# Expert tiles of a routed layer moved from a stage of their own into the chunks of a gated recurrence

## The chip, the cores and the metric

The kernel runs on one core of one Trainium2 chip. The metric is the device time of one execution in microseconds, lower is better. Five engines work beside each other, each through its own instructions in a fixed order: TensorE (PE in the profile, with its weight loads shown as PEld), VectorE (DVE), ScalarE (ACT), GpSimd (POOL) and SyncE (SP). SP and ACT start plain transfers, POOL starts those whose rows are picked by a list of indices; 16 DMA engines carry them all.

## The reference

A gated linear recurrence feeds a routed two-expert layer. For each of 4 batches and 8 heads, over 768 steps with head size 48:

```python
state = alpha[:, :, t, :, None] * state + einsum('bhd,bhe->bhde', k[:, :, t], v[:, :, t])
y[:, :, t] = einsum('bhd,bhde->bhe', q[:, :, t], state)
```

The result is laid out as x with 3072 rows (tokens) of 384. Then, with 8 experts of hidden size 1024:

```python
noisy = x @ w_gate + log1p(exp(x @ w_noise)) * noise      # 3072 x 8
top2, weights = two largest per row, softmax over the two
out[row] = sum over its two experts e: weight * (relu(x[row] @ w1[e]) @ w2[e])
```

All in float32.

## The kernel before

**Recurrence.** The 3072 rows are 24 chunks of 128 steps, six to a batch. For a chunk, `prepare` turns alpha, k and q so that steps lie along the free axis (12 transposes, line 197), takes the running product of alpha with a scan (line 211), and scales q by it and k by its reciprocal (lines 214 to 218). `scores` multiplies k and q within the chunk (line 230), keeps the lower triangle (line 232) and turns k back (line 236). `finish` carries the state from chunk to chunk (lines 247 to 257), forms y (lines 260 and 265), stores its 128 rows to `x_rows` in DRAM and turns y for the router (`put_x`). The loop runs ahead of itself: in round n stand `load(n+3)`, `prepare(n+2)`, `scores(n+1)` and `finish(n)`.

**Router.** After every third chunk, which closes a unit of 384 rows (8 units), `router` works out the two experts of each row, their weights, and the place of each row in its expert's list: `rank` (lines 515 and 516) counts how many earlier rows chose the same expert. It writes six groups of 128 entries of 16 bytes (row number, weight, two further row numbers) into `table` in DRAM with transfers from POOL (line 527). Each expert owns 3072 rows of the table. A row number of 6144 means "none", and the whole table is filled with it at the start (`clear_table`, one transfer on ACT's queue). `half_rows` in DRAM holds the first of a row's two results until the second arrives, and is filled with zeros at the start (`clear_half`, eight transfers on SP's queue).

**Plan.** After the last chunk, `plan_tiles` turns the eight counts into a list of 55 tiles of up to 128 rows: for each its expert and its first place in the table.

**Experts.** Then 55 tiles run one after the other. For a tile, SP reads the expert's number and the place from the plan and loads 128 table entries (`tab`) and the expert's w1 (1.5 MB, three buffers); POOL gathers the rows of x (`gather_x`, line 596, four buffers); PE turns them (`turn_x`, line 603), forms the hidden layer in two halves (line 616: 24 products, each shown as two records), and the output (line 623: 8 products); ACT scales it by the row's weight. In `combine` POOL fetches the stored halves (line 635), stores first halves (line 641) and writes finished rows (line 649). All of w2 (12 MB) stays on chip, loaded in eight transfers from round n = 2 on.

A tile framework builds the program. Its list scheduler sets the order of each engine's instructions from the order in the source and from when operands should be ready, and it places all waits; no order is written by hand. Stages that are opened one after the other with their own buffer pools share memory, and here the experts' pools open after the recurrence's have closed. At the end a branch, not taken with this data, redoes everything with a general form of the recurrence.

Of the kernel before, what the change touches and what calls it, by code (L numbers as in the profile page):

```python
# [18 lines left out]
def kernel(  # L19
# [23 lines left out]

    nc = tc.nc
# [3 lines left out]
    C = 128  # L48
# [13 lines left out]
    RMAX = N  # L62
    NTILE = (2 * N) // C + E - 1
    TROWS = E * RMAX + (E + 0) * C
    NONE = 2 * N
    RANGE = 1e-18

# [22 lines left out]
    expert_ids = const.tile([C, E], F32, name="expert_ids")  # L90
    region = const.tile([C, E], F32, name="region")
    for e in range(E):
        nc.gpsimd.memset(expert_ids[:, e:e + 1], float(e))
        nc.gpsimd.memset(region[:, e:e + 1], float(e * RMAX))
# [7 lines left out]
    tile_no = const.tile([1, NTILE], F32, name="tile_no")  # L102
    nc.gpsimd.iota(tile_no, pattern=[[1, NTILE]], base=0, channel_multiplier=0, allow_small_or_imprecise_dtypes=True)
    step_no = const.tile([1, RMAX // C], F32, name="step_no")
    nc.gpsimd.iota(step_no, pattern=[[C, RMAX // C]], base=0, channel_multiplier=0,
# [6 lines left out]
    nothing = const.tile([C, TROWS // C * 4], U32, name="nothing")  # L112
    nc.gpsimd.memset(nothing, NONE)
    zeros = const.tile([C, NT // 8, DM], F32, name="zeros")
    nc.gpsimd.memset(zeros, 0.0)

    def clear_table():
        nc.scalar.dma_start(out=table.rearrange("(p r) w -> p (r w)", p=C), in_=nothing)

    def clear_half():  # L120
        for i in range(8):
            nc.sync.dma_start(out=half_rows.rearrange("(i n p) d -> i p n d", i=8, p=C)[i], in_=zeros)

    NIN = 3
# [28 lines left out]
    def put_x(n, y, on, ps_tp, xT, at):  # L153
        y_sb = on.tile([C, DM], F32, name="y_sb")
        nc.scalar.copy(y_sb, y.rearrange("p h d -> p (h d)"))
        tp = ps_tp.tile([C, NP, C], F32, tag="tp", name="tp")
        for a in range(KO):
            nc.tensor.transpose(tp[:, a, :], y_sb[:, ds(a * C, C)], ident)  # L158
        nc.scalar.copy(xT[:, :, ds(at * C, C)], tp[:, 0:KO, :])
        nc.sync.dma_start(out=x_rows[ds(n * C, C), :], in_=y_sb)  # L160


    def fast_gla(es, after):
        gc = pool("gc", 1, es)
        vp = pool("vp", 4, es)
        kp = pool("kp", 2, es)
        sp = pool("sp", 2, es)
        xtp = pool("xtp", 2, es)
        rp = pool("rp", 2, es)
        ps_sc = pool("ps_sc", 1, es, space=PS)  # L170
        ps_tp = pool("ps_tp", 3, es, space=PS)
        ps_y = pool("ps_y", 3, es, space=PS)
        ins = {x: [gc.tile([C, H, DP], F32, name=f"{x}_in{i}") for i in range(NIN)] for x in "akq"}
# [4 lines left out]
        a_s = [gc.tile([C, NP, C + 1], F32, name=f"a_s{i}") for i in range(2)]  # L178
        P_s = [gc.tile([C, NP, C + 1], F32, name=f"P_s{i}") for i in range(3)]
        for t in a_s:  # L180
            nc.vector.memset(t[:, :, 0:1], 0.0)
        least = gc.tile([C, NP, C + 1], F32, name="least")
        nc.vector.memset(least, RANGE)
        nc.vector.memset(least[:, :, 0:1], 1.0)
        P_end = gc.tile([C, NT, NP], F32, name="P_end")
        above = gc.tile([C, NT], F32, name="above")
        less_1 = gc.tile([C, 1], F32, name="less_1")
        nc.vector.memset(less_1, -1.0)
        MTs = [gc.tile([C, 2, NP, C], F32, name=f"MT{i}") for i in range(2)]
# [3 lines left out]

        def transposed(src):
            tp = ps_tp.tile([C, NP, C], F32, tag="tp", name="tp")
            for j in range(NP):
                nc.tensor.transpose(tp[:, j, :], src[:, 2 * j:2 * j + 2, :], ident)  # L197
            return tp

        def prepare(n):  # L200
            c = chunks[n]
            a_t = transposed(ins["a"][n % NIN])
            nc.scalar.copy(a_s[n % 2][:, :, 1:C + 1], a_t)  # L203
            over_1 = kp.tile([C, NP, C], F32, name="over_1")
            nc.scalar.activation(over_1, a_t, AF.Relu, bias=less_1, accum_out=above[:, n:n + 1])
            k_t = transposed(ins["k"][n % NIN])
            k_raw = kp.tile([C, NP, C], F32, name="k_raw")
            nc.scalar.copy(k_raw, k_t)
            q_t = transposed(ins["q"][n % NIN])
            P = P_s[n % 3]  # L210
            nc.vector.tensor_tensor_scan(P.rearrange("p j t -> p (j t)"), a_s[n % 2].rearrange("p j t -> p (j t)"),  # L211
                                         least.rearrange("p j t -> p (j t)"), 0.0, op0=ALU.mult, op1=ALU.max)
            c["q"] = kp.tile([C, NP, C], F32, name="q_P")
            nc.vector.tensor_mul(c["q"], q_t, P[:, :, 1:C + 1])
            over = kp.tile([C, NP, C], F32, name="over")
            nc.vector.reciprocal(out=over, in_=P[:, :, 1:C + 1])  # L216
            c["k"] = kp.tile([C, NP, C], F32, name="k_P")
            nc.gpsimd.tensor_tensor(c["k"], k_raw, over, op=ALU.mult)  # L218
            nc.gpsimd.tensor_copy(out=P_end[:, n, :, None], in_=P[:, :, C:C + 1])
            c["end"] = kp.tile([C, NP, 2], F32, name="end")  # L220
# [3 lines left out]
        def scores(n):  # L224
            c = chunks[n]
            sc = [ps_sc.tile([C, NP, C], F32, tag=f"sc{i}", name=f"sc{i}") for i in range(2)]
# [6 lines left out]
            if n % NCH != NCH - 1:  # L233
                tp = ps_tp.tile([C, NP, C], F32, tag="tp", name="tp")
                for j in range(NP):
                    nc.tensor.transpose(tp[:, j, :], c["k"][:, j, :], ident)  # L236
                c["k_end"] = kp.tile([C, NP, C], F32, name="k_end")
                nc.scalar.copy(c["k_end"], tp)

        def finish(n, xT, at):  # L240
            c = chunks.pop(n)
            first, last = n % NCH == 0, n % NCH == NCH - 1
            y = ps_y.tile([C, H, D], F32, tag="y", name="y")
            if not last:
                s1 = ps_y.tile([C, NP, 2, D], F32, tag="y", name="s1")
                for j in range(NP):
                    nc.tensor.matmul(s1[:, j], c["k_end"][:, j, :], c["v"][:, 2 * j:2 * j + 2, :], start=True,  # L247
                                     stop=True)
                S_new = kp.tile([C, NP * 2, D], F32, name="S_new")
                end = c["end"].rearrange("p j i -> p (j i)")[:, :, None].to_broadcast([C, NP * 2, D])  # L250
                s1 = s1.rearrange("p j i d -> p (j i) d")
                if first:
                    nc.vector.tensor_mul(S_new, s1, end)
                else:
                    S_sum = kp.tile([C, NP * 2, D], F32, name="S_sum")
                    nc.vector.tensor_add(S_sum, chunks["S"], s1)
                    nc.gpsimd.tensor_tensor(S_new, S_sum, end, op=ALU.mult)
            if not first:
                for j in range(NP):
                    nc.tensor.matmul(y[:, 2 * j:2 * j + 2, :], c["q"][:, j, :], chunks["S"][:, 2 * j:2 * j + 2, :],  # L260
                                     start=j == 0, stop=False, skip_group_check=True)
# [5 lines left out]
            if not last:  # L267
                chunks["S"] = S_new
            put_x(n, y, sp, ps_tp, xT, at)

        def load(n):
            chunks[n] = {"v": load_chunk(n, ins, vp)}

        load(0)
        load(1)
        prepare(0)
        load(2)
        prepare(1)
        scores(0)
        for n in range(NT):  # L280
            if n + 3 < NT:
                load(n + 3)
            after(n)
            if n + 2 < NT:
                prepare(n + 2)
            if n + 1 < NT:
                scores(n + 1)
            if n % UC == 0:
                xT = xtp.tile([C, KO, UT], F32, name="xT")
            finish(n, xT, n % UC)  # L290
            if n % UC == UC - 1:
                router(n // UC, xT, rp, ps_y)


        out_of = rp.tile([C, 4], F32, name="out_of")
        nc.vector.tensor_reduce(out=out_of[:, 0:1], in_=P_end.rearrange("p n j -> p (n j)"), axis=mybir.AxisListType.X,
                                op=ALU.min)
        nc.vector.tensor_reduce(out=out_of[:, 1:2], in_=above, axis=mybir.AxisListType.X, op=ALU.max)
        nc.vector.tensor_scalar(out=out_of[:, 2:3], in0=out_of[:, 0:1], scalar1=2 * RANGE, scalar2=None, op0=ALU.is_lt)
        nc.vector.tensor_scalar(out=out_of[:, 3:4], in0=out_of[:, 1:2], scalar1=0.0, scalar2=None, op0=ALU.is_gt)  # L300
        count = ps_y.tile([C, 2], F32, tag="y", name="count")
        nc.tensor.matmul(count, ones, out_of[:, 2:4], start=True, stop=True)
        again = rp.tile([1, 1], F32, name="again")
        nc.vector.tensor_reduce(out=again, in_=count[0:1, :], axis=mybir.AxisListType.X, op=ALU.add)
        nc.vector.tensor_copy(out=again_i, in_=again)
        plan_tiles(rp, ps_y)


    def general_gla(es):
# [4 lines left out]
        sp = pool("g_sp", 2, es)  # L314
# [407 lines left out]
```

## Time and profile before

| | |
|---|---|
| time, median of 3 runs | 980.18 us (979.2 to 986.29) |
| the profiled execution | 982.83 us, of which its span is 981.1 us |
| TensorE busy | 879.0 us, 90% of the span |
| VectorE, ScalarE, GpSimd busy | 268.1, 200.4, 347.9 us |
| mean granted TensorE clock | 0.866 |
| recurrence, router and plan | from 0 to about 370 us |
| 55 expert tiles | from about 370 to 971 us |

The profile cuts the span into 40 slices of 24.5 us and gives the busy share of each engine in tenths, and likewise the TensorE clock that was granted. Groups of instructions are named by line, engine and operation, output tile, input tiles. A table by windows gives, for each stretch, the busy time of each engine with the number of its instructions in brackets, the granted clock, the share of the DMA engines' time and the GB/s.

### The profile page before, as it was taken

Reading aid. Unit: us, or ns where it says so; the run is one execution under the profiler, and the core shown is the slowest. Engines: PE = TensorE matmul, PEld = TensorE weight load, DVE = VectorE, ACT = ScalarE, POOL = GpSimd, SP = SyncE. Lnnn points to the kernel's source line nnn. Section 1 sums busy time; section 2 is a strip of 40 time slices with the busy share of each in tenths; the row PEclk is TensorE's granted clock in tenths of the full one; section 3 lists DMA queues with packets and bytes.
Section 4 is the critical chain, followed back from the end, with each engine's and each line's share of the span. In section 5 each row is a group of like instructions: output and inputs, shape, how many; then the busy total and the mean of one; then the engine's idle time right before and its main releaser. Section 6 shows DMA issues by size and latency. Waiting matters only on the chain.

```text
span 981.1 us, 14593 instructions
## 1 busy us (share of the span) xinstructions
PE 879.0 (90%) x5393; PEld 738.9 (75%) x5393; DVE 268.1 (27%) x544; ACT 200.4 (20%) x370; POOL 347.9 (35%) x412
## 2 busy tenths in 40 slices
PE   5987879898797609999999999999999999999995
PEld 4876778797697607788788878887887788778873
DVE  7844584755855200011010101010101010101010
ACT  2412241333332201111111111111111111111110
POOL 3213143242342223344334433443444343434322
PEclk9955595676875558999999999999999999999998
DMA  9999162343410027544554555556555655665420
GB/s 236 292 371 211 32 128 56 66 97 63 84 41 9 17 74 264 210 169 157 195 203 156 172 203 192 176 176 217 193 179 185 216 196 180 198 218 168 160 66 3
DMA packets 164463, 152.85 MB, mean 156 GB/s; under 512 B 121704, under 2 KB 137755, under 8 KB 164384
## 3 DMA queue, kind: packets, MB, share of 16 engines
q1 hardware_dynamic: 144736, 127.53, 42.0%
q0 software_dynamic: 15616, 23.76, 7.2%
q10 hardware_dynamic: 4032, 0.53, 0.3%
q8 instruction: 46, 0.75, 0.3%
q14 instruction: 33, 0.27, 0.1%
HBM read 139.83 MB, written 31.57 MB: 175 GB/s over the span
## 4 chain that ended last, share of the span: by engine, by line
issue 44%; PE 22%; POOL 18%; DMA 7%; DVE 4%; ACT 2%; POOLq 1%; ACTq 0%; DVEq 0%; SPq 0%
POOL prev L635 6%; DMA half_rows<-o,tab 5%; POOL x_in L596 5%; PE y L265 5%; PE sc L230 4%; POOL out_dram L649 3%; PE tp L197 3%; PE s L247 3%; PE y L260 2%; PE lg L464 2%; POOL half_rows L641 2%; DVE over L216 1%; PE tp L158 1%; POOL table L527 1%; PE tp L236 1%
## 5 line engine op out<-in xcount | busy, mean ns | idle before, releaser
L616 PEld LDWEIGHTS h_ps<-xt,w 128*128 128x128 f32 x2640 | 304.8, 193 | 15.4 <-DVE xt L605 1.1
L616 PE MATMUL h_ps<-xt,w 128*128 128x128 f32 x2640 | 305.2, 276 | 0.7 <-DVE xt L605 0.7
L623 PE MATMUL o_ps<-w,h 128*128 x880 | 292.9, 486 | 0.0
L623 PEld LDWEIGHTS o_ps<-w,h 128*128 128x128 f32 x880 | 162.9, 190 | 102.0
L641 POOL DMA_INDIRECT half_rows<-o,tab x55 | 66.5, 1210 | 269.6 <-ACT o L634 263.4
L618 ACT ACTIVATE h<-h_ps 128x512 f32<-128x512 f32 x110 | 65.7, 597 | 265.6 <-PE h_ps L616 265.6
L648 DVE TENSOR_TENSOR both<-o,prev 128x384 f32<-128x384 f32 x55 | 30.8, 559 | 294.1 <-ACT o L634 281.3
L605 DVE COPY xt<-x_ps 128x384 f32<-128x384 f32 x55 | 30.7, 559 | 268.9 <-PE x_ps L603 268.9
L634 ACT ACTIVATE o<-o_ps,tab 128x384 f32<-128x384 f32 x55 | 32.0, 581 | 268.8 <-PE o_ps L623 268.8
L527 POOL DMA_INDIRECT table<-entry,place_u x48 | 48.7, 1015 | 104.7 <-DMA table<-entry,place_u 61.8
L216 DVE RECIPROCAL over<-P_s 128x512 f32<-128x512 f32 x24 | 80.4, 3348 | 0.6
L596 POOL DMA_INDIRECT x_in<-x_rows,tab x55 | 56.0, 1018 | 50.9 <-PE x_ps L603 38.3
L230 PE MATMUL sc<-q_P,k_P 48*128 48x128 f32 x384 | 50.7, 379 | 23.7 <-DVE den L486 10.2
L635 POOL DMA_INDIRECT prev<-half_rows,tab x55 | 58.3, 1059 | 38.4 <-DMA half_rows<-o,tab 28.4
L230 PEld LDWEIGHTS sc<-q_P,k_P 48*128 48x128 f32 x384 | 40.6, 260 | 33.3 <-issue 11.5
L265 PE MATMUL y<-vt,MT 128*128 128x48 f32 x384 | 65.5, 340 | 0.0
L265 PEld LDWEIGHTS y<-vt,MT 128*128 128x128 f32 x384 | 64.9, 262 | 0.1
L649 POOL DMA_INDIRECT out_dram<-both,tab x55 | 55.5, 1010 | 18.1 <-issue 16.5
L218 POOL TENSOR_TENSOR k_P<-k_raw,over 128x512 f32<-128x512 f32 x24 | 31.2, 1302 | 61.6 <-DVE over L216 23.5
L603 PE MATMUL x_ps<-ident,x_in 128*128 128x128 f32 x165 | 27.4, 276 | 28.5 <-DMA x_in<-x_rows,tab 28.5
L211 DVE TENSOR_TENSOR_SCAN P_s<-a_s,least 128x516 f32<-128x516 f32 x24 | 32.0, 1334 | 52.8 <-ACT a_s L203 52.7
L603 PEld LDWEIGHTS x_ps<-ident,x_in 128*128 128x128 f32 x165 | 20.1, 143 | 28.6 <-DMA x_in<-x_rows,tab 28.6
(119 smaller groups left out, 627.6 us busy)
## 6 DMA issues: line engine op xcount, KB each, us to landing
w<-in_moe_w_dram SPq DMA_DIRECT2D x63, 1536.0 KB
a_in<-in_alpha_dram SPq DMA_DIRECT2D x24, 192.0 KB
k_in<-in_k_dram SPq DMA_DIRECT2D x24, 192.0 KB
q_in<-in_q_dram SPq DMA_DIRECT2D x24, 192.0 KB
vt<-in_v_dram SPq DMA_DIRECT2D x24, 192.0 KB
half_rows<-zeros SPq DMA_DIRECT2D x8, 576.0 KB
x_rows<-y_sb SPq DMA_DIRECT2D x24, 192.0 KB
tab<-table SPq DMA_DIRECT2D x55, 2.0 KB
```

Of the source, the lines that this page charges most:

```text
L216: nc.vector.reciprocal(out=over, in_=P[:, :, 1:C + 1])
L230: nc.tensor.matmul(sc[i][:, j, :], c["k"][r, j, :], c["q"][r, j, :], start=True, stop=True)
L265: nc.tensor.matmul(y[:, h, :], MTs[n % 2][:, i, j, :], c["v"][:, h, :], start=first and h == 0, stop=h == H - 1, skip_group_check=True)
L527: nc.gpsimd.indirect_dma_start(out=table, out_offset=bass.IndirectOffsetOnAxis(ap=place_u[:, i:i + 1], axis=0), in_=entry.bitcast(U32)[:, ...
L596: nc.gpsimd.indirect_dma_start(out=x_in[i % NB], out_offset=None, in_=x_rows, in_offset=bass.IndirectOffsetOnAxis(ap=tabs[i][:, 0:1], axis=0),
L603: nc.tensor.transpose(x_ps[:, a, :], x_in[i % NB][:, ds(a * C, C)], ident)
L616: nc.tensor.matmul(h_ps[:, fo, :], w1[:, a, ds((half * FO // 2 + fo) * C, C)], xt[:, a, :], start=a == 0, stop=a == KO - 1)
L618: nc.scalar.activation(h[:, ds(half * FO // 2, FO // 2), :], h_ps, AF.Relu)
L623: nc.tensor.matmul(o_ps, h[:, fo, :], w2[:, ds(e, 1), fo, :].rearrange("p o d -> p (o d)"), start=fo == 0, stop=fo == FO - 1)
L635: get = nc.gpsimd.indirect_dma_start(out=prev[i % 2], out_offset=None, in_=half_rows, in_offset=bass.IndirectOffsetOnAxis(ap=tab[:, 3:4], ...
L641: put = nc.gpsimd.indirect_dma_start(out=half_rows, out_offset=bass.IndirectOffsetOnAxis(ap=tab[:, 2:3], axis=0), in_=o, in_offset=None, b ...
L649: put = nc.gpsimd.indirect_dma_start(out=out, out_offset=bass.IndirectOffsetOnAxis(ap=tab[:, 3:4], axis=0), in_=both, in_offset=None, boun ...
```

## The change

The expert tiles no longer wait for all counts. After each unit, `plan_tiles(u)`, some 25 small VectorE instructions, hands out a fixed number of tiles from the counts so far, always such tiles as are already full; the number (`GIVEN`) is what 8 experts must have full whatever the counts are: 0, 5, 11, 17, 23, 29, 35 after units 0 to 6, and all 55 after the last. `given` notes for each tile how many rows of each expert earlier tiles hold, so that a row's entry, which now has the other expert and the place there, tells whether the other result came first: five small VectorE instructions per tile (`gather_x`). One round of the chunk loop from n = 7 on holds two tiles, their four steps (`tile_steps`) laid between the seven steps of the chunk; 33 tiles stand in the loop, 22 after it. Recurrence and experts now live at the same time, so buffers go down: `NIN` 3 to 2, w1 3 to 2, x_in 4 to 3, transposes in PSUM 3 to 2, y in PSUM 3 to 1. `x_rows` is stored from ACT's queue. Both clears are one transfer each on ACT's queue with a source that repeats 16 and 512 bytes, 25600 and 9216 pieces. w2 is loaded from round 1 on. Entry transfers no longer wait for each other. `get_half` stands ahead of the second layer. The router's logits are formed per chunk and kept in `lgs`.

The core of the diff (new code in the order of the file):

```diff
+    EV = E + 1
+    GIVEN = [max(0, (2 * UT * (u + 1) - E * (C - 1) + C - 1) // C) for u in range(NU - 1)] + [NTILE]
...
-    nothing = const.tile([C, TROWS // C * 4], U32, name="nothing")
-    zeros = const.tile([C, NT // 8, DM], F32, name="zeros")
+    nothing = const.tile([C, 4], F32, name="nothing")
+    zeros = const.tile([C, C], F32, name="zeros")
     def clear_table():
-        nc.scalar.dma_start(out=table.rearrange("(p r) w -> p (r w)", p=C), in_=nothing)
+        cleared = nc.scalar.dma_start(out=table.bitcast(F32).rearrange("(p r) w -> p r w", p=C),
+                                      in_=nothing[:, None, :].to_broadcast([C, TROWS // C, 4]))
...
+    def put_entries(place, entry):
+        put = nc.gpsimd.indirect_dma_start(
+            out=table, out_offset=bass.IndirectOffsetOnAxis(ap=place, axis=0), in_=entry, in_offset=None,
+            bounds_check=TROWS - 1, oob_is_err=False)
+        for earlier in entries[1:] + taken:
+            tc.declare_no_dep(put.ins, earlier, reason="different rows of the table")
+        tc.add_manual_dep(put.ins, entries[0].name, AFTER, reason="the table is cleared first")
...
     def clear_half():
-        for i in range(8):
-            nc.sync.dma_start(out=half_rows.rearrange("(i n p) d -> i p n d", i=8, p=C)[i], in_=zeros)
+        nc.scalar.dma_start(out=half_rows.rearrange("(p n) (a d) -> p (n a) d", p=C, d=C),
+                            in_=zeros[:, None, :].to_broadcast([C, NT * KO, C]))
-    NIN = 3
+    NIN = 2
...
-        nc.sync.dma_start(out=x_rows[ds(n * C, C), :], in_=y_sb)
+        nc.scalar.dma_start(out=x_rows[ds(n * C, C), :], in_=y_sb)
...
+    def plan_tiles(u, on):
...
+        lo, hi, last, now = GIVEN[u - 1] if u else 0, GIVEN[u], u == NU - 1, u + 1
...
         def gather_x(i, units):
+            tab = tabs[i]
...
+            nc.vector.scalar_tensor_tensor(other, expert_ids, tab[:, 2:3], given[:, i, 0:E], op0=ALU.is_equal,
+                                           op1=ALU.mult, accum_out=before_it)
...
+            nc.vector.memset(skip[:, 0:1], 0.0)
+            nc.vector.tensor_tensor(skip[:, 1:2], tab[:, 3:4], before_it, op=ALU.is_lt)
+            nc.vector.tensor_tensor(skip[:, 2:3], tab[:, 3:4], before_it, op=ALU.is_ge)
...
+            nc.vector.scalar_tensor_tensor(wheres[i], skip, float(NONE), tab[:, 0:1].to_broadcast([C, 3]),
+                                           op0=ALU.mult, op1=ALU.add)
+            nc.gpsimd.indirect_dma_start(out=x_in[i % NB], out_offset=None, in_=x_rows[0:units * UT, :],
+                                         in_offset=bass.IndirectOffsetOnAxis(ap=wheres[i][:, 0:1], axis=0),
...
+    def tile_steps(i, do, units):
+        def first():
+            load_w1(i + 1)
+            if i + 2 < units[1]:
+                gather_x(i + 2, units[0])
+            layer1(i, 0)
+        def second():
+            layer1(i, 1)
+        def third():
+            if i + 1 < units[1]:
+                turn_x(i + 1)
+            get_half(i)
+            layer2(i, 0)
+        def fourth():
+            layer2(i, 1)
+            combine(i)
...
-        fast_gla(es, after)
-        experts(es)
+        def start_batch(u):
+            lo = GIVEN[u - 1] if u else 0
+            for i in range(lo, min(lo + 4, GIVEN[u])):
+                load_tab(i)
+            load_w1(lo)
+            for i in range(lo, min(lo + 2, GIVEN[u])):
+                gather_x(i, u + 1)
+            turn_x(lo)
...
+        for n in range(NT):
+            u = (n - 4) // UC
+            chunk = [lambda: prepare(n + 2), lambda: load(n + 3), lambda: scores(n + 1), lambda: state(n),
+                     lambda: output(n), lambda: turn_y(n), lambda: route(n)]
+            if n == 0:
+                load_router()
+                clear_table()
+                clear_half()
+            if n == 1:
+                load_w2()
+            work = []
+            if n >= 4 and GIVEN[u] > (GIVEN[u - 1] if u else 0):
+                lo = GIVEN[u - 1] if u else 0
+                if (n - 4) % UC == 0:
+                    start_batch(u)
+                part = (n - 4) % UC
+                for i in range(lo + 2 * part, min(lo + 2 * part + 2, GIVEN[u])):
+                    work += steps_of(i)
...
+            for j in range(max(len(work), len(chunk))):
+                if j < len(work):
+                    work[j]()
+                if j < len(chunk):
+                    chunk[j]()
+        for i in range(tiles, NTILE):
+            ...
```

## The prediction, made before the changed kernel was run

> **What bounds the kernel now.** I read the slices first, then windows of 5 us, then the timeline around the joint of the two stages.
>
> ```profile
> span 981.1 us, 14593 instructions
> ...
> PE   5987879898797609999999999999999999999995
> ...
> PEclk9955595676875558999999999999999999999998
> ```
>
> Slices 1 to 15 are the recurrence: TensorE is never idle long, yet at about half clock. Slices 16 to 40 (24.5 us each) are the tiles: TensorE full, at full clock. The windows show what the clock means for the recurrence; in them the columns are the stretch, its length, then busy us and count of PE, PEld, DVE, ACT, POOL, and last clock, DMA share, GB/s.
>
> ```profile
> 35.00:40.00 5.00, 5.00 (x49) 4.68 (x48) 2.73 (x5) 0.80 (x2) 2.07 (x2) 1.00 1.04 221
> ...
> 60.00:65.00 5.00, 5.00 (x26) 5.00 (x25) 1.25 (x2) 0.00 (x0) 2.16 (x3) 0.50 1.07 372
> ...
> 225.00:230.00 5.00, 0.25 (x2) 0.25 (x2) 4.93 (x29) 1.96 (x3) 1.40 (x2) 0.75 0.00 1
> 230.00:235.00 5.00, 5.00 (x25) 5.00 (x25) 2.39 (x9) 0.00 (x0) 2.06 (x3) 0.50 0.01 0
> ```
>
> Both 35 to 40 and 60 to 65 count as fully busy, but with 49 records against 26: full clock is 0.102 us a record, half clock 0.192. At 225 TensorE stands while VectorE does the router's 29 small instructions; after that wait the clock is 0.50. So the recurrence pays twice, in waits and in clock.
>
> ```profile
> 39.10 26.52 SPq L150 DMA_DIRECT2D w<-in_moe_w_dram  x8
> ...
> 338.76 0.59 PE L515 MATMUL rank<-chosen,before 128*128 128x24 f32 x2 [4.66 <-DVE entry L489]
> ...
> 369.58 0.90 PE L603 MATMUL x_ps<-ident,x_in 128*128 128x128 f32 x3 [28.50 <-DMA x_in<-x_rows,tab]
> ...
> 947.67 5.52 PE L616 MATMUL h_ps<-xt,w 128*128 128x128 f32 x48
> ...
> 958.52 5.52 PE L616 MATMUL h_ps<-xt,w 128*128 128x128 f32 x48
> ```
>
> A tile takes 958.52 - 947.67 = 10.85 us of TensorE, 55 take 597. Between the last `rank` and the first turned tile lie 30.8 us, 28.5 of them idle. And SP was held 26.5 us by eight w2 loads (12.6 MB; 33.8 us at the 372 GB/s of the window at 60): whoever issues a long transfer stands until most of it has gone.
>
> **The work itself.** All tiles are 597 us. The recurrence has about 1673 records (288 + 80 + 72 transposes, 384 + 384 + 160 + 160 + 144 products from the groups' counts), 69.7 a chunk: 7.1 us at 0.102. Were TensorE never to wait, 24 x 7.1 + 597 = 767 us. The change removes the joint and lets tile products fill the recurrence's waits; the built order of TensorE's instructions does show them alternating from round 7 on, so that it does what it says is not in doubt. The question is what new waits it brings. I go along TensorE's path.
>
> **A. Until `rank` of unit 1 (113.7 us in the trace of before): 129 us.** New here is that both clears stand in ACT's queue, ahead of the recurrence's first copies, in small pieces.
>
> ```profile
> q1 hardware_dynamic: 144736, 127.53, 42.0%
> ...
> q10 hardware_dynamic: 4032, 0.53, 0.3%
> ```
>
> The table's clear is 25600 pieces, 1600 on each of 16 engines. Queue q10 (noise and router weights, 32 bytes a piece) gives 0.25 to 0.35% of 16 x 981 us over 4032 packets, 10 to 14 ns each: 16 to 22 us. Queue q1's mean (42% over 144736) is 46 ns, as its packets are larger: 73 us as the upper end. I take 19, since size is what q10 shares with it. As SP was held by w2, ACT is held: its copies, which begin at 9.5 us in before, begin at about 30 (7.8 where the clear is issued now, 19, and some 3 for loads beside it). Three copies later the half-row clear holds it again: 4.7 MB at 372 GB/s are 13 us, and 10 us of SP's loads share the way, less what stays queued: free at 48. On SP's queue the third q load waits for these copies, and five w2 pieces (4.2 us each) stand behind it and ahead of chunk 4's alpha, which is copied by ACT at 78 instead of 40.0. From there to `rank` of unit 1 before took 113.7 - 40.0 = 74, of which the copies of chunks 5 and 6 (47.2 and 83.2) lay 36 apart, not the usual 13 (40 a unit): w2 again, 23 us that are now paid already. So 78 + 51 = 129.
>
> By the Trainium skill ("DMA: Bandwidth & Descriptors", Specifications), writes under 512 bytes are done as read and modify, which speaks against clearing in 16-byte pieces; the rows show only small reads, and the page has no price for it. If it doubled the 19 us, the sum would grow by about as much.
>
> **B. From there to the first turned tile: 150.** The chain that took 30.8 us before holds six entry transfers, each waiting for the last.
>
> ```profile
> POOL table L527 <- DMA table<-entry,place_u: 61.8, 29, 5.8
> ...
> x_in<-x_rows,tab POOLq DMA_INDIRECT x55, 6.4
> ...
> table<-entry,place_u POOLq DMA_INDIRECT x48, 3.4
> ```
>
> Issued from 342.4 to 359.2, they took 16.8; now 6 x 1.0 us. Five small VectorE steps come in (0.16 each, 0.8). 30.8 - 10.8 + 0.8 = 20.8 us, beside which TensorE has two chunks' remainders.
>
> **C and D. 16 chunks x 7.1 = 114 and 55 tiles x 10.85 = 597.** In a round stand two tiles and a chunk, 28.8 us. Hidden beside it, from the groups: VectorE 7.2 for the chunk, 2 x 1.9 for tiles with the new steps, some 3 for router and plan; POOL 2 x 4.3 transfers, 2.3 for the chunk, 2 for entries; DMA 0.53 (its share between 500 and 600) x 21.7, and 5.8 for a chunk's loads (0.56 and 0.31 of 25 us from 200 to 250, 3.75 chunks), 17 us. The `x_rows` stores leave SP, where one stood 4.2 us behind w2 at 65.7, for ACT, where an issue takes under 1 us. Each has room, so w1 in two buffers (freed after a first layer, due two half layers and a chunk later, 16 us at least, for 1.5 MB, 4.2 us) and gathers (6.4 us, issued more than a tile ahead) should arrive. The recurrence runs a round ahead of need, so its scan and reciprocal have 28 us. If that cover goes, each late gather costs its remainder to everything behind it, since one queue serves both.
>
> **E. New waits: 49.** (1) `rank`: from where ACT takes the logits, 334.14, to `rank` took 4.6 us, and now with one more copy 4.9; ahead of it stand four second-layer products (2.7). 2.2 us in each of 6 units, and 1.6 for the clock after it (the first 48 records of a tile at 371 took 7.09 us instead of 5.52): 23. (2) The last batch starts after two tiles, 21.7 us, against a chain of 20.8 behind other work of POOL: 2. (3) Small waits in a round, from fewer buffers (one y, two for transposes) and mixed queues, that no row shows: 0 to 5 us, from nothing (all operands a round early) to one `rank`-like wait; nearest are the 0 to 1 us idle entries of most groups: 1.5 x 16 = 24.
>
> **F. Tail: 12,** as before (969.2 to 981.1: last output, two transfers, the branch).
>
> Sum: 150 + 114 + 597 + 49 + 12 = 922 us of span, 924 as a profiled execution (982.8 against 981.1). The median was 2.7 below that execution, so **921 us**, 6% faster.
>
> **Rivals.**
>
> *Clock, slower than before.* If TensorE's short waits in each round keep the clock low, the shared stretch (33 tiles and 16 chunks, 472 us at full clock) grows. Against it speaks that the first tile lost only those 1.6 us; for it that 60 to 65 is fully busy and yet at 0.50. It decides once an eighth of the stretch is at half rate, 59 us. At a quarter: 921 + 118 = 1040. The skill ("TensorE: Matmul & The Clock Gate", Part 1) says that some 3.4 us of sustained work restore full clock; by that the sum loses nothing here, while the stretch from 60 to 80 us, busy at 0.50, does not follow it.
>
> *The clears hold ACT longer, or the waits move.* At 46 ns a piece the table takes 73 instead of 19 us: 975. Or every round waits 5 us, by POOL's queue, where a fetch of halves waits for the last store to land (2.6 us) ahead of gathers: 921 + 56 = 977. Either is no measurable gain.
>
> *Better.* w2 arrives while ACT is held, so A could be 15 us shorter, and E could be 15: 870.
>
> **Numbers.** Forecast (895 to 955) 0.43; better 0.17; the second rival (955 to 1000) 0.18; the clock 0.22. Within 1% is about what a measurement here can tell from no change, 970 to 990. Faster by more: 0.43 + 0.17 + 0.07 = 0.67; same 0.07; slower 0.04 + 0.22 = 0.26. Range 868 to 1025: below it lies little, above it half of the clock's rival.
>
> **What would show it.** ACT's first copy near 30 us and chunk 4's near 78; the first turned tile near 150; rounds of 29 to 31 us at a granted clock over 0.95; `rank` waits of 2 us; no idle before the last batch over 3 us; a tile at 10.85 in the last 22. Wrong if rounds take over 33 us, if the clock in them is below 0.9, or if the first copy comes after 60.

## The result, and the profile after

The changed kernel takes **1052.63 us** (1041.2 to 1056.08) against 979.69 us (976.91 to 986.29) for the kernel before on the same chip: ratio 1.0714, 95% interval 1.0616 to 1.0812. It is 7% slower, where 921 us was forecast and the range ended at 1025. The profiled execution took 1056.08 us, its span 1054.2.

First the page of the changed kernel: the span, two rows of the slices (now 26.4 us each) and the queue that carries the clears (packets, MB, share of 16 engines' span).

```profile
span 1054.2 us, 15008 instructions
...
PE   1100487988997999899799999998998799999995
...
PEclk9999755555997899899989989997999899999998
...
q10 hardware_dynamic: 42192, 9.97, 12.4%
```

In the first four slices TensorE does next to nothing. The stretch of low clock, slices 3 to 15 in the kernel before, is now slices 5 to 10, and tiles follow, so the change does what it says; but the tiles start 100 us later than forecast. Queue q10 took 0.3% of the engines' time before, and now 12.4%.

The same stretch by windows (stretch, length, then busy us and count of PE, PEld, DVE, ACT, POOL; clock, DMA share, GB/s):

```profile
25.00:50.00 25.00, 3.09 (x20) 2.50 (x20) 1.33 (x2) 0.00 (x0) 0.00 (x0) 1.00 1.81 29
50.00:75.00 25.00, 0.00 (x0) 0.00 (x0) 0.00 (x0) 0.00 (x0) 0.00 (x0) 1.00 1.33 66
75.00:100.00 25.00, 0.00 (x0) 0.00 (x0) 0.00 (x0) 0.00 (x0) 0.00 (x0) 1.00 1.56 20
```

From 50 to 100 all five engines stand. Only the DMA engines work, at a share of 1.3 to 1.8 (above 1, since the recorded times of single transfers overlap), and they move 20 to 66 GB/s; in the kernel before it was 276 GB/s over the first 100 us. What ACT and SP do meanwhile stands in their timelines (start, us, queue, line, operation; the length of an issue is how long it held its engine):

```profile
27.66 74.32 ACTq L153 DMA_DIRECT2D half_rows<-zeros  x1
102.08 0.58 ACT L242 COPY a_s<-tp 128x512 f32<-128x512 f32 x1 [93.26 <-issue]
```

```profile
29.68 10.73 SPq L167 DMA_DIRECT2D vt<-in_v_dram  x1
...
47.07 9.85 SPq L165 DMA_DIRECT2D q_in<-in_q_dram  x1
108.77 0.37 SPq L165 DMA_DIRECT2D a_in<-in_alpha_dram  x1
```

ACT's issue of the half rows' clear lasts 74.32 us, behind the table's pieces (the same 9216 pieces took 0.59 us to issue in wide_table below, where they went first). SP has each 192 KB load on its hands for 6 to 11 us (0.4 to 0.7 later on), then stands until the table's clear has landed, 103.9 us after its issue.

Further on, in TensorE's timeline, these lines answer to those of the kernel before:

```profile
228.74 0.62 PE L536 MATMUL rank<-chosen,before 128*128 128x24 f32 x2
...
250.50 0.90 PE L672 MATMUL x_ps<-ident,x_in 128*128 128x128 f32 x3 [0.61 <-DMA x_in<-x_rows,where]
...
944.63 5.52 PE L683 MATMUL h_ps<-xt,w 128*128 128x128 f32 x48
...
955.47 5.52 PE L683 MATMUL h_ps<-xt,w 128*128 128x128 f32 x48
```

`rank` of unit 1 comes at 228.74 (forecast 129), the first turned tile at 250.50 (forecast 150), and a tile of the last batch takes 10.84 us. So two differences make up the 132 us between the span and the forecast span of 922: 100 before the first tile, and, from there to the end, 803.7 instead of 772, 32.

The 32 us lie between 250.5 and 824.5, where the last 20 tiles begin: 574 us, of which 35 tiles and 16 chunks were to take 379.8 + 113.6 = 493.4. Of the 80.6 us beyond, TensorE is idle for 39.5 and "busy" for 41.1 too long. Its idle time by what ended it (line, releaser, total us, times, longest), and the whole stretch as a window:

```profile
PE y L305 <- DVE S_sum L293: 10.4, 2, 5.3
PE x_ps L672 <- DMA x_in<-x_rows,where: 10.2, 4, 5.9
PE rank L536 <- ACT o L712: 7.9, 6, 1.3
```

```profile
250.50:824.50 574.00, 534.53 (x3487) 445.89 (x3488) 209.89 (x688) 130.71 (x258) 227.61 (x262) 0.94 0.55 172
```

With two more entries of the list (5.2 and 4.9 us), TensorE waits 20.5 us for the state that y needs. How that comes about shows in one unit, VectorE first, then TensorE:

```profile
329.85 0.23 DVE L654 SCALAR_TENSOR_TENSOR other<-expert_idv,tab,given 128x8 f32<-128x8 f32 x1 [4.25 <-DMA tab<-table]
...
332.96 0.55 DVE L293 TENSOR_TENSOR S_sum<-S,s 128x384 f32<-128x384 f32 x1
```

```profile
333.56 2.02 PE L305 MATMUL y<-S,q_P 128*128 128x96 f32 x8 [5.32 <-DVE S_sum L293]
```

VectorE stands at the first of the five new steps of a gather, since the tile's table rows have not landed; the state's sum is queued behind these steps; TensorE waits for the sum. In windows of 5 us from 330 to 350 the clock is 0.69, 0.50, 0.50, 0.60, and 1.00 after that: the wait of 5.3 us, which ends at 333.56, is followed by some 15 us of work at about half clock. It is not always so long: after the wait of 5.0 us in the unit at 521 the windows show 0.50 from 526 to 531, 0.77 to 536 and then 1.00.

### The profile page after: what moved, and what is told of

Its sections match the earlier page's. It is cut to its first block, busy times and chain, and to the rows that moved or that the text cites. A ratio compares the mean times of both kernels' runs of the same rounds, so it can differ in the third digit from the quotient of the medians.

```text
span 1054.2 us, 15008 instructions
## 1 busy us (share of the span) xinstructions
PE 876.1 (83%) x5405; PEld 727.1 (69%) x5405; DVE 321.2 (30%) x973; ACT 202.3 (19%) x394; POOL 350.3 (33%) x444
## 3 DMA queue, kind: packets, MB, share of 16 engines
q10 hardware_dynamic: 42192, 9.97, 12.4%
## 4 chain that ended last, share of the span: by engine, by line
PE 43%; issue 17%; DMA 13%; ACTq 7%; DVE 7%; POOL 6%; ACT 3%; SPq 2%; another core or an unknown queue 1%; POOLq 0%; DVEq 0%
PE h_ps L683 14%; PE o_ps L695 12%; ACTq L153 7%; DMA table<-entry,place_u 5%; PE y L310 4%; DVE over L254 2%; PE tp L234 2%; DMA a_in<-in_alpha_dram 2%; PE sc L269 2%; DMA k_in<-in_k_dram 2%; PE y L305 2%; POOL prev L702 2%; DMA half_rows<-o,where 2%; POOL x_in L663 2%; PE lg L202 1%
## 5 line engine op out<-in xcount | busy, mean ns | idle before, releaser
L683 PE MATMUL h_ps<-xt,w 128*128 128x128 f32 x2640 | 326.9, 283 | 0.0
L713 POOL DMA_INDIRECT half_rows<-o,where x55 | 65.1, 1183 | 189.2 <-ACT o L712 186.1
L663 POOL DMA_INDIRECT x_in<-x_rows,where x55 | 56.3, 1024 | 116.8 <-PE x_ps L672 68.3
L719 DVE TENSOR_TENSOR prev<-prev,o 128x384 f32<-128x384 f32 x55 | 30.6, 556 | 183.7 <-ACT o L712 166.9
L254 DVE RECIPROCAL over<-P 128x512 f32<-128x512 f32 x24 | 80.4, 3352 | 1.6
L702 POOL DMA_INDIRECT prev<-half_rows,where x55 | 59.5, 1082 | 52.9 <-DMA half_rows<-o,where 32.6
L248 DVE TENSOR_TENSOR_SCAN P<-a_s,least 128x516 f32<-128x516 f32 x24 | 30.4, 1267 | 131.4 <-ACT a_s L242 131.1
L234 PEld LDWEIGHTS tp<-ident,q_in 128*128 128x128 f32 x96 | 13.2, 173 | 82.5 <-ACT tp L243 78.4
L720 POOL DMA_INDIRECT out_dram<-prev,where x55 | 55.4, 1007 | 22.9 <-issue 14.6
L271 DVE COPY_PREDICATED MT<-upto,sc 128x512 f32<-128x512 uint32 x48 | 32.7, 723 | 47.9 <-PE sc L269 45.8
L255 POOL TENSOR_TENSOR k_P<-k_P,over 128x512 f32<-128x512 f32 x24 | 30.6, 1273 | 49.8 <-DVE over L254 36.3
```

What stands on the lines that cost most here:

```text
L663: nc.gpsimd.indirect_dma_start(out=x_in[i % NB], out_offset=None, in_=x_rows[0:units * UT, :], in_offset=bass.IndirectOffsetOnAxis(ap=wher ...
L683: nc.tensor.matmul(h_ps[:, fo, :], w1[:, a, ds((part * FO // 2 + fo) * C, C)], xt[:, a, :], start=a == 0, stop=a == KO - 1)
L702: get = nc.gpsimd.indirect_dma_start(out=prev[i % 2], out_offset=None, in_=half_rows, in_offset=bass.IndirectOffsetOnAxis(ap=wheres[i][:, ...
L713: put = nc.gpsimd.indirect_dma_start(out=half_rows, out_offset=bass.IndirectOffsetOnAxis(ap=where[:, 1:2], axis=0), in_=o, in_offset=None, ...
L720: put = nc.gpsimd.indirect_dma_start(out=out, out_offset=bass.IndirectOffsetOnAxis(ap=where[:, 2:3], axis=0), in_=prev[i % 2], in_offset=N ...
```

## The experiments

All times are medians in us; "profiled" is the profiled execution alone, where there was one run. The kernel before had medians of 976.8 to 980.5 beside them.

| kernel | us | ratio to before, 95% interval |
|---|---|---|
| wide_clears | 980.14 | 0.9984 (0.9943 to 1.0025) |
| wide_table | 974.87 profiled | |
| before_table | 1073.69 profiled | |
| before_both | 1087.53 profiled | |
| piece_64, piece_32 | 989.16, 991.55 profiled | |
| piece_16_apart | 1016.37 profiled | |
| wide_order | 985.11 | 1.0042 (1.0008 to 1.0076) |
| wide_shift | 944.00 | 0.9611 (0.9537 to 0.9686) |
| shift | 1023.13 profiled | |
| shift_spread | 939.82 | 0.9608 (0.9539 to 0.9677) |
| best | 934.59 | 0.9508 (0.9444 to 0.9571) |

### The clears in wider pieces

```diff
-    nothing = const.tile([C, 4], F32, name="nothing")
+    nothing = const.tile([C, 40, 4], F32, name="nothing")
-        cleared = nc.scalar.dma_start(out=table.bitcast(F32).rearrange("(p r) w -> p r w", p=C),
-                                      in_=nothing[:, None, :].to_broadcast([C, TROWS // C, 4]))
+        cleared = nc.scalar.dma_start(out=table.bitcast(F32).rearrange("(p a r) w -> p a (r w)", p=C, r=40),
+                                      in_=nothing.rearrange("p r w -> p (r w)")[:, None, :].to_broadcast([C, TROWS // C // 40, 40 * 4]))
```

and likewise `zeros` of 192 instead of 128 numbers a partition (wide_clears); the table alone (wide_table).

> The changed kernel with both clears written from wider pieces: 640 bytes (640 pieces) for the table, 768 bytes (6144 pieces) for the half rows; nothing else. Theory 1 (ACT is held by the table's 25600 small pieces): ACT's second set of copies comes near 15 to 25 us instead of 102, rank of unit 1 near 130 to 140 us instead of 229, the stretch from the first turned tile to the end stays at 804 us, and the time falls by 90 to 110 us to 945 to 965. Theory 2 (the small pieces only happen to cover a wait that the loads of w2 would impose anyway): at most 40 us come back, 1010 to 1050.

> Only the table's clear in pieces of 640 bytes, the half rows' clear stays in 9216 pieces of 512 bytes. If the 16-byte pieces alone are the cause, within 10 us of the kernel with both clears wide (945 to 970). If the 512-byte pieces matter as well, half of the gain or less: about 1000.

Between the two theories: the profiled execution falls by 81 us, from 1056.08 to 975.35 (the median of its runs is 980.14). The first turned tile comes at 166.2 instead of 250.5, and the stretch from there to the end stays, 807.2 us for 803.7, as the first theory has it. TensorE and ACT in wide_clears:

```profile
143.85 0.62 PE L536 MATMUL rank<-chosen,before 128*128 128x24 f32 x2
...
166.16 0.90 PE L672 MATMUL x_ps<-ident,x_in 128*128 128x128 f32 x3 [1.15 <-DMA x_in<-x_rows,where]
```

```profile
27.52 0.59 ACT L242 COPY a_s<-tp 128x512 f32<-128x512 f32 x1 [17.70 <-DMA half_rows<-zeros]
```

What is missing is in the early part: `rank` of unit 1 at 143.9, not 130 to 140, as ACT still stood 17.7 us, until 27.5, for the half rows' clear. With the table alone, in one run, the time is the same within 1 us, so the 16-byte pieces were all that the wider clears cured. The wider clears only bring the kernel level with the one before.

### The small pieces in the kernel before

The same small pieces at the old place in the kernel before; SP keeps the half rows' clear (before_table), or ACT gets both (before_both):

```diff
-        nc.scalar.dma_start(out=table.rearrange("(p r) w -> p (r w)", p=C), in_=nothing)
+        nc.scalar.dma_start(out=table.rearrange("(p r) w -> p r w", p=C),
+                            in_=nothing[:, None, :].to_broadcast([C, TROWS // C, 4]))
```

> The kernel before, with the table's clear in 25600 pieces of 16 bytes at its old place in ACT's queue; the half rows stay with SP in large pieces, and ACT has no second transfer to issue behind it. If what costs is that ACT is held in its next issue, little changes: 980 to 995. If the small pieces slow every other transfer on the 16 DMA engines, the chunks' loads come late and it takes 1030 to 1070.

> The kernel before, with both clears as in the changed kernel: one transfer each on ACT's queue, 25600 pieces of 16 bytes and 9216 of 512. If the clears alone explain the late start, the recurrence ends 75 to 105 us later and the time is 1055 to 1085. If the late start needs the rest of the change (two load buffers, w2 a round earlier), 980 to 1010.

My theory that ACT is held fell here. In before_table ACT issues nothing behind the clear and goes on at once, and yet the time is 95 us above the 978.34 of the kernel before. TensorE's list of waits says for what (its columns are as above):

```profile
PE tp L198 <- DMA k_in<-in_k_dram: 44.8, 4, 16.8
...
PE tp L198 <- DMA a_in<-in_alpha_dram: 27.2, 6, 10.1
PE tp L198 <- DMA q_in<-in_q_dram: 23.6, 4, 13.4
```

These are 95.6 us of waiting for the chunks' loads, the whole loss. The DMA queues of its first 110 us (packets, MB, share):

```profile
q10 hardware_dynamic: 29504, 0.53, 102.2%
```

29504 packets in 1.022 x 16 x 110 us are 61 ns each on average. The small pieces keep the 16 engines for 100 us, whether ACT is held behind them or not. In before_both, where ACT is held for 71.3 us too, the wait is put down to ACT (66.2 us), but the time is only 14 us more. Two things hold up before_table's loads: while the pieces are written, SP's issues and the landings are slow, and from 68 on SP waits 42 us for the table's landing before its next issue:

```profile
56.52 11.26 SPq L134 DMA_DIRECT2D k_in<-in_k_dram  x1
109.83 0.37 SPq L134 DMA_DIRECT2D q_in<-in_q_dram  x1
```

TensorE's waits up to 101 us, 78.7 of the 95.6, are all for loads issued before SP's stand; only the last 17 or so, from the q load at 109.83 on, come after it. So most of the loss is the slow loads.

### How small is too small

The table in 6400 pieces of 64 bytes, in 12800 of 32, and in the 25600 of 16 but with each partition's pieces 2048 bytes apart:

```diff
-        cleared = nc.scalar.dma_start(out=table.bitcast(F32).rearrange("(p r) w -> p r w", p=C),
+        cleared = nc.scalar.dma_start(out=table.bitcast(F32).rearrange("(r p) w -> p r w", p=C),
```

> The changed kernel with the table's clear in 6400 pieces of 64 bytes instead of 25600 of 16 bytes; nothing else. If a small write costs by the piece (60 ns each, as the 16-byte pieces took), 6400 of them take 24 us on 16 engines and the time is 975 to 990. If it costs by the byte, 96 us as before: 1045 to 1060. If only writes under some size between 16 and 64 bytes are slow, 970 to 980.

> The changed kernel, its table cleared in the same 25600 pieces of 16 bytes, but each partition's pieces 2048 bytes apart in the table instead of side by side. If a 16-byte write is slow because its neighbours in the same few dozen bytes are in flight at the same time, the pieces take 9 to 15 ns and the time is 975 to 990. If each write below 64 bytes is slow by itself, the clear takes 95 us as before: 1045 to 1060.

> The changed kernel with the table's clear in 12800 pieces of 32 bytes. 64-byte pieces took 11 ns each and 16-byte pieces 60. If only pieces that share 64 bytes with a neighbour are slow, 32-byte pieces lie between: 20 to 40 ns each, 16 to 32 us for the clear, 990 to 1020. If 32 bytes is enough for a fast write, 985 to 992, as with 64 bytes.

The trace's records of single transfers give a mean of 11.1 ns a piece at 64 bytes, 9.1 at 32, and at 16 bytes 59.8 side by side in the changed kernel and 30.2 apart. So the price goes neither by the piece nor by the byte. Nor is it a price that each 16-byte piece pays: the median is 9 ns there too, side by side and apart. Side by side 83% of the pieces took under 20 ns, and the 14% that took over 100 ns hold some 85% of the time; at 32 and 64 bytes next to none took that long. The 192-byte packets of SP's loads in the same stretch (17.5 to 117 us) behave alike: a median of 15 ns as in the kernel before, but a mean of 76 instead of 16. It is a number of long stalls, and both queues have them. The time of piece_64, 989.16, lies in the range that was given for a price by the piece, but its ground, 60 ns a piece, is refuted. 32 bytes are enough for a fast write: piece_32 met its second expectation. At 16 bytes the order of the places accounts for half; apart, a piece is on average still three times as dear as one of 32 bytes, so neither expectation of piece_16_apart was met (1016.37). In that run the piece beside each one belongs to the next partition, so neighbours can still have been in flight together: that they cause the stalls is neither shown nor ruled out. What makes 16 bytes special stays open.

### The waits for the table's rows

First, the order alone: each gather's steps stand behind the state's sum of their round, all else as in wide_clears.

```diff
+            for gather in ahead:
+                tc.add_manual_dep(gather, summed.ins.name, AFTER, reason="the state first")
```

> The changed kernel with wide clears, and the five small VectorE steps of each gather put behind the state's sum of the same round by an explicit order; tiles begin when they did. Theory 1 (the state's sum stands queued behind steps that wait for table rows): TensorE's waits of y for the state (15 us with wide clears) fall to 5 or less; if the rows then come in time for the tiles, the time is 950 to 965. Theory 2 (the wait is for the rows themselves, whoever stands behind them): the wait turns up ahead of the first turned tile of each unit, as waits of x_ps for its gather (6 us with wide clears, then 15 to 30), and the time stays at 970 to 990.

The second theory held. VectorE's waits for `tab` in the shared stretch fall to 4.9 us (56.0 in wide_clears, 71.6 in the changed kernel); first the changed kernel, then wide_order:

```profile
DVE other L654 <- DMA tab<-table: 71.6, 14, 9.0
```

```profile
DVE other L656 <- DMA tab<-table: 4.9, 4, 4.3
```

Yet the time is 985.11, nothing gained. TensorE's waits between 178 and 753 us:

```profile
PE x_ps L674 <- DMA x_in<-x_rows,where: 25.7, 8, 6.8
...
PE y L307 <- DVE S_sum L293: 2.7, 3, 1.1
```

The wait for the state is down to 2.7 us (15.0 in the same stretch of wide_clears, in three entries), and the wait for the gathered rows has grown from 3.6 to 25.7: it was a wait for the rows all along. What is too short is the time from a unit's `rank` to its first tile. So next, each unit's tiles one round later, with wide clears (wide_shift) and with the 16-byte clear (shift):

```diff
-            u = (n - 4) // UC
+            u = (n - 5) // UC
-            if n >= 4 and GIVEN[u] > (GIVEN[u - 1] if u else 0):
+            if n >= 5 and GIVEN[u] > (GIVEN[u - 1] if u else 0):
...
-                if (n - 4) % UC == 0:
+                if (n - 5) % UC == 0:
-                part = (n - 4) % UC
+                part = (n - 5) % UC
```

> The changed kernel with wide clears, and each unit's tiles begun one round later (two rounds after the unit's last chunk instead of one), so that the table rows of a tile have landed when VectorE comes to the five small steps of its gather. Theory 1 (in each unit VectorE stands 4 to 8 us at those steps, waiting for the rows, with the state's sum of the chunk queued behind it, TensorE idles about 5 us for that sum and then runs about as much again at half clock): the waits of y for the state (15 us with wide clears) and the wait ahead of the last batch (some 9 us) go, the clock in the shared stretch rises from 0.94 to 0.97 or more, and one chunk more runs without tiles beside it (7 to 13 us): 935 to 955. Theory 2 (these waits only stand in for others, such as rank or the gathers of x): 965 to 985.

> The changed kernel as it is, 16-byte clear included, and only each unit's tiles begun one round later. If the two causes are independent (the clear delays the start by some 75 us, the short distance between a unit's last chunk and its tiles costs some 30 us), 1015 to 1030. If the late start already covers part of the waits for table rows, 1040 to 1055.

944.00 and, in one run, 1023.13, both within the first expectation. The profiled executions fall by 29.7 and by 33.0 us, with wide clears and without, so the two causes add up. TensorE's waits between 179 and 713 us, and a window of one unit (six tiles, three chunks):

```profile
PE rank L536 <- DVE den L515: 4.7, 4, 1.2
PE y L305 <- DVE S_sum L293: 4.2, 3, 2.2
```

```profile
302.00:392.00 90.00, 88.80 (x619) 73.87 (x619) 38.35 (x116) 23.51 (x47) 40.63 (x46) 1.00 0.62 187
```

Idle time in the stretch falls from 41.6 (wide_clears, 166.2 to 741) to 13.2 us. The window, at full clock and nearly without waits, shows what a chunk costs beside tiles: (88.8 - 6 x 10.85) / 3 = 7.9 us.

### Two steps further

w2 two experts a round in rounds 1 to 4 (shift_spread), and besides, the half rows' clear issued behind the stores of two chunks (best):

```diff
-            if n == 1:
-                load_w2()
+            if 1 <= n <= 4:
+                load_w2(n)
...
+            tc.add_manual_dep(cleared.ins, behind.name, AFTER, reason="later")
```

> As the kernel with wide clears and the later start of tiles, and w2 loaded two experts a round in rounds 1 to 4 instead of all eight in round 1. If what is left of the late start (first turned tile at 166 instead of 150 with wide clears) is that SP stands behind w2 ahead of the chunks' loads, the tiles start 10 to 20 us earlier: 920 to 940. If TensorE's half clock in the first chunks sets their pace, no more than 5 us against the run with the later start of tiles.

> As the kernel with wide clears, the later start of tiles and w2 over rounds 1 to 4, and the half rows' clear issued only behind the stores of the chunks 0 and 1, so that it neither holds ACT for 18 us nor shares the DMA engines with the first chunks' loads. If that hold is what is left of the late start, ACT's second set of copies comes near 12 us instead of 27, the tiles start 10 to 18 us earlier, 922 to 932. If TensorE's half clock in the first chunks sets their pace, or the clear only collides with w2 instead, 935 to 945.

shift_spread's profiled execution is 4.8 us below that of wide_shift, with the first tile at 174.1 instead of 178.9; the ratios are the same, which is the second expectation. (Its source also places the half rows' clear in round 3, but ACT issues it at 6.3 us, as in wide_shift.) SP's stand behind w2 was not what is left of the late start. In best, ACT's copies for chunk 1 do come early:

```profile
11.81 0.59 ACT L245 COPY a_s<-tp 128x512 f32<-128x512 f32 x1 [1.86 <-PE tp L237]
```

and the first tile stands at 153.95, 20 us earlier than in shift_spread, but the profiled execution falls by only 4.7 (the median is 934.59; by the ratios it is 1%, with intervals that overlap): `rank` of the units 3 to 6 now follow each other in 95.6, 98.9 and 96.9 us, 90.2 to 92.8 in wide_shift. Waits of `tp` for ACT (9.8 us) and a clock of 0.95 to 0.98 in these windows are part of that; why this order of the work has them was not settled. So the time lies between the two expectations, 922 to 932 and 935 to 945, and met neither. Best is 4.9% faster than the kernel before (interval 4.3 to 5.6), and 11% faster than the changed kernel.

## Why the prediction was wrong

**Step A failed, by 100 us of the 132.** It took a piece of the table's clear at 10 to 14 ns, from a queue of 32-byte pieces, "since size is what q10 shares with it". But those were reads into the chip's memory, and 32 bytes; 16-byte writes to DRAM took 60 ns on average, and even the bound of 46 ns was too low. The step put the long stalls, which hold most of that time, at nothing; the other pieces, at 9 ns, are near what q10 had shown. The clear's 19 us were 104 to its landing. The mechanism put on it, "as SP was held by w2, ACT is held", is real (74.32 us at line 153) and not the point: before_table loses as much with ACT free, since the chunks' loads are slow while the pieces are written. With that, the cover counted on fell too. w2 was to arrive while ACT is held, "23 us that are now paid already"; but its issue stands on SP, which stood as well, and only one of the eight loads had been issued by 108 us. Chunk 4's alpha was copied at 159.6, not 78, and from there to `rank` it took 69, not 51.

By the Trainium skill ("DMA: Bandwidth & Descriptors", Specifications), writes under 512 bytes are read and modified first. I wrote that the sum "would grow by about as much" as the 19 us if it doubled them, and left it out; it pointed the right way. But the runs do not show it at that threshold: 32-byte writes took 9.1 ns, no more than the 32-byte reads of the router's loads (8.9 to 13.2), and only at 16 bytes came the stalls.

**Step B held:** 21.8 us from `rank` to the first turned tile, forecast 20.8. The six entry transfers no longer wait for each other: they take 7.4 us (forecast 6) instead of 16.8.

**C and D:** a tile was right to 0.01 us; a chunk beside tiles takes 7.9 (in wide_shift's window), not 7.1, which is 13 us in 16 chunks and was counted nowhere.

**Step E was mis-sized,** 81 us for 49, those 13 among them. Its idle time came out almost right, 39.5 us for 39, and that is luck. `rank` waits 7.9 us in six units, 13 forecast. "Small waits in a round", which no row had shown, were 24 us, and the last batch 2; 31 were measured for the state and the gathers, from a cause that was named for the last batch alone: "the last batch starts after two tiles, 21.7 us, against a chain of 20.8". Every unit runs this race, behind the other work of POOL and VectorE, and loses it by 2 to 8 us. What was mis-sized is the time at a low clock behind such waits: 10 us forecast, after `rank` alone, and some 28 lost (41.1 less the chunks' 13; a remainder, not a measurement).

**F held:** 12 us from the last output product to the end.

**The rivals.** The second one named the clears and was closest: "46 ns a piece" was its price, 60 the measured mean. The clock rival did not decide: what was lost to it in the shared stretch, 28 us, is about half of the 59 us from which it would. It shows in part after each wait. Of the marks, "if the first copy comes after 60" was not met by its letter: chunk 0's copies still came at 7.08, ahead of the hold; but chunk 1's came at 102. From one unit's `rank` to the next, three rounds with six tiles, it took 92 to 99 us, so rounds were 31 to 33 us, at a mean clock of 0.94 in the stretch, where 29 to 31 and over 0.95 were forecast.

## What to carry to other kernels

Before a transfer is cut into small pieces, count them and look for a row of the same direction and size: 25600 writes of 16 bytes kept the 16 DMA engines for 100 us and slowed every other load in that time, and a source of 640 bytes per piece cured it for 0.6 KB a partition. Where a change lets work follow its condition closely, time the chain between them in every round, not only in the first and last; one round more of distance was worth 30 us. A wait put down to one instruction may only stand ahead of another: an order that removed it showed where it really was.

## What the runs showed of the hardware

Writes of 16 bytes to DRAM took 59.8 ns each on average side by side (the changed kernel) and 30.2 ns with each partition's pieces 2048 bytes apart (piece_16_apart), those of 32 bytes 9.1 ns (piece_32). The median was 9 ns in all three: the difference lies in stalls, pieces over 100 ns, 14% of them side by side and 7% apart. 64 bytes took 11.1 ns (piece_64), 512 bytes 27 to 43 in the runs with the half rows' clear in such pieces. While the 16-byte pieces ran, all traffic together came to 16 to 31 GB/s (before_table, 25 to 100 us). And a wait of 5.3 us on TensorE was followed by some 15 us of uninterrupted work at a granted clock of 0.50 to 0.60 (the changed kernel, 335 to 350).
